# Pooled attention and two MoE layers in one kernel: another distance, order and buffering of a pair's preparation

## The chip, the cores and the metric

The kernel runs on one core of a Trainium2 chip. Its engines are TensorE (PE, with PEld its weight loads), VectorE (DVE), ScalarE (ACT) and GpSimd (POOL); SyncE (SP) issues the transfers (DMAs). Each engine works through its own list of instructions in order and waits at the first whose inputs or buffers aren't ready. The metric is the device time of one execution in microseconds (us), the median of several runs.

## The reference

```python
def _attn_ref(q, k, v):                       # [4, 8, 1152, 64] each
    q_pool = q.reshape(B, H, S // 2, 2, D).mean(axis=3)
    scores = scale * np.matmul(q_pool, k.transpose(0, 1, 3, 2))
    scores = scores - np.max(scores, axis=-1, keepdims=True)
    attn = np.exp(scores)
    attn = attn / (np.sum(attn, axis=-1, keepdims=True) + 1e-09)
    return np.matmul(attn, v)                 # -> x [2304, 512]

def _moe_ref(x, w_in, w_out):                 # 512 -> 2048 -> 512
    h = x @ w_in
    return (h - np.tanh(h)) @ w_out

def _moe2_ref(x, w_in, w_out, s, b):
    r = np.maximum(x @ w_in, 0.0)
    return (s * (r * r) + b) @ w_out
```

All inputs are float32. The output is _moe2_ref of _moe_ref of the attention.

## The kernel before

The 32 heads are worked in 16 pairs, n = 0 to 15, and in a pair the heads j = 0 and 1 follow one another. A head has nine key tiles t of 128 keys, and its 576 pooled queries are two halves g of 288. Keys and queries are kept as a rounded high part and a low remainder, so one tile of scores s is two matmuls: the high parts (L343, operands T1 and U1) and the cross terms together with minus the row's maximum (L344, operands T2 and U2; the last row of U2 is −max, tile c). ACT takes the exponential into pf (L345). After every three tiles a batch of 12 matmuls pv adds pf times values (L412); the sum of pf over keys is made on TensorE in pairs 0 to 3 (su, L378), and afterwards mostly on GpSimd, which adds tiles of pf into acc (L399), with a short su at the end (L425).

Before a pair is scored, the generator prep(n) makes its operands. It adds pairs of queries (L258, on GpSimd after pair 0), transposes queries (ptq, L263) and keys (ptk, L280) on TensorE, copies the results to U1 and T1 on ACT and takes the low parts ql and kl on VectorE. The two heads come out of the transposes one above the other, so halves are moved by DMA: U1 (L275, L276), T1 (L289) and the low parts of the keys into T1 (L290, L291, "T<-kl"). After a pause of GAP ticks come the maxima: 27 tiles of products ptm (L304, L305, L308), each reduced by VectorE (L309), then a reduction over the partial maxima m, a transpose ptc (L313) and a copy with sign changed to c (L314). prep_head(n, j) fills U2, T2 and the values vo by DMA (L324 to L326) and, when c is there, its row of U2 (L332, L334, "U<-c").

The order of the work comes from ticks. The main loop steps through pairs, heads and tiles; every tile has four ticks, a pair 72, and at each tick every prep in the list goes on to its next yield. A scheduler then fixes each engine's list from the order in which instructions were written and from their priorities. Beside the attention stand conversions of the MoE weights on VectorE and GpSimd (L189 to L204), and from pair 5 on matmuls of the first MoE layer (h, L478; y, L491), which fill TensorE. Tiles of scores have three PSUM buffers, and ptq, ptk, ptm and ptc share three others. Behind the attention, from about 700 us, stand the rest of the first MoE layer (L651, L662) and the second (L651, L724).

Of the kernel before, what the change touches and what calls it, by code (L numbers as in the profile page):

```python
# [52 lines left out]
def attention_moe_moe_kernel(  # L53
# [196 lines left out]
    def prep(n):  # L250

        T1, Uz, ql = T1s[n % 2], U1s[n % 2], qls[n % 2]
        U1 = [Uz[j][:, QOFF[j]:QOFF[j] + SQ] for j in range(2)]
        ops[n] = (T1, U1)

        for j in range(2):
            eng = dve if n == 0 else pool
            eng.tensor_add(qr[:, :, 0, j * D:(j + 1) * D], qr[:, :, j, 0:D], qr[:, :, j, D:2 * D])  # L258
        yield 4
        for g in range(2):  # L260
            pt = psP.tile([P, KB], F32, tag="pp", name=f"ptq{n}_{g}")
            for i in range(3):
                nc.tensor.transpose(  # L263
                    pt[:, i * QP:(i + 1) * QP],
                    qr[:, 3 * g + i, 0],
                    ident[:QP, :QP],
                )
            act(U1[1][:, g * HB:(g + 1) * HB], pt[:, :HB], AF.Copy)
            yield 1
            dve.tensor_sub(  # L270
                ql[:, g * HB:(g + 1) * HB], pt[:, :HB], f32(U1[1][:, g * HB:(g + 1) * HB])
            )
            yield 1
        for i in range(2):
            dma(out=f32(U1[0][i * D:(i + 1) * D, :]), in_=f32(U1[1][0:D, :]))  # L275
        dma(out=f32(U1[1][0:D, :]), in_=f32(U1[1][D:P, :]))  # L276
        for g in range(NKB):
            pt = psP.tile([P, KB], F32, tag="pp", name=f"ptk{n}_{g}")
            for i in range(3):
                nc.tensor.transpose(  # L280
                    pt[:, i * P:(i + 1) * P],
                    kr[:, 3 * g + i].rearrange("p h d -> p (h d)"), ident)
            act(T1[1][:, g * KB:(g + 1) * KB], pt, AF.Copy)
            yield 1
            dve.tensor_sub(
                kl[:, g * KB:(g + 1) * KB], pt, f32(T1[1][:, g * KB:(g + 1) * KB])
            )
            yield 1
# [497 lines left out]
```

## Time and profile before

| | |
|---|---|
| median of 3 runs | 1451.95 us (1451.56 to 1452.4) |
| profiled execution | 1451.74 us |
| its span in the trace | 1450.0 us |
| mean granted TensorE clock, whole span | 0.978 |
| busy: PE, DVE, ACT, POOL | 1376.4, 869.2, 553.2, 384.0 us |
| share of the span | 95%, 60%, 38%, 26% |

The span is the time from the first to the last instruction that the profiler recorded; the profiled execution's own time holds 1.74 us around it. Busy shares are means over the whole span, and the attention and the MoE stages have different limits. A granted clock of 1.00 is 2.4 GHz and 0.50 is 1.2 GHz; a value between them over a stretch means that part of it ran at either.

### The profile page before, as it was taken

Reading aid. Unit: us, or ns where it says so; the run is one execution under the profiler, and the core shown is the slowest. Engines: PE = TensorE matmul, PEld = TensorE weight load, DVE = VectorE, ACT = ScalarE, POOL = GpSimd, SP = SyncE. Lnnn points to the kernel's source line nnn. Section 1 sums busy time; section 2 is a strip of 40 time slices with the busy share of each in tenths; the row PEclk is TensorE's granted clock in tenths of the full one; section 3 lists DMA queues with packets and bytes.
Section 4 is the critical chain, followed back from the end, with each engine's and each line's share of the span. In section 5 each row is a group of like instructions: output and inputs, shape, how many; then the busy total and the mean of one; then the engine's idle time right before and its main releaser. Section 6 shows DMA issues by size and latency. Waiting matters only on the chain.

```text
span 1450.0 us, 23111 instructions
## 1 busy us (share of the span) xinstructions
PE 1376.4 (95%) x8670; PEld 1157.0 (80%) x8670; DVE 869.2 (60%) x1638; ACT 553.2 (38%) x1360; POOL 384.0 (26%) x311
## 2 busy tenths in 40 slices
PE   5999989999999999999999998899999999999998
PEld 4656656776777777776898997899889989989987
DVE  7967795756656655668797289934973332323332
ACT  2434435544545444444332233333333222223232
POOL 1211145655655555555221033100220000000000
PEclk9989989999999999999999999999999999999999
DMA  8656654645557535544688044644612020201000
GB/s 200 166 133 152 164 131 116 148 120 116 148 127 168 119 96 127 118 120 114 204 263 263 2 139 149 205 143 149 208 60 66 0 66 0 66 4 62 1 22 22
DMA packets 157647, 169.62 MB, mean 117 GB/s; under 512 B 52064, under 2 KB 130016, under 8 KB 157536
## 3 DMA queue, kind: packets, MB, share of 16 engines
q1 hardware_dynamic: 157536, 168.15, 42.6%
q8 instruction: 68, 1.11, 0.3%
q14 instruction: 43, 0.35, 0.1%
HBM read 101.98 MB, written 30.67 MB: 91 GB/s over the span
## 4 chain that ended last, share of the span: by engine, by line
PE 71%; DVE 16%; DMA 8%; issue 2%; ACT 2%; POOL 1%; SPq 1%; DVEq 0%; ACTq 0%; POOLq 0%
PE h L651 19%; PE o L724 14%; PE pv L412 8%; PE ptm L308 6%; PE y L662 5%; PE s L344 4%; PE s L343 4%; PE y L491 3%; PE h L478 3%; DVE t L193 2%; DMA T<-kl 2%; DVE t L189 2%; DMA raw<-in_moe_w_in_dram 2%; DVE t L191 2%; PE su L425 2%
## 5 line engine op out<-in xcount | busy, mean ns | idle before, releaser
L651 PE MATMUL h<-xx,w 128*128 128x288 f32 (+1 forms) x2328 | 388.4, 316 | 1.8 <-DVE thb L505 1.7
L651 PEld LDWEIGHTS h<-xx,w 128*128 128x128 f32 x2328 | 365.6, 189 | 11.0 <-DVE thb L505 2.7
L309 DVE TENSOR_REDUCE mp<-ptm 128x1 f32<-128x384 f32 x432 | 220.4, 548 | 169.9 <-PE ptm L308 162.3
L345 ACT ACTIVATE pf<-s 128x288 f32<-128x288 f32 x576 | 218.8, 411 | 201.8 <-PE s L344 194.9
L204 POOL TENSOR_TENSOR w<-t,w 128x512 fp32r<-128x512 f32 (+1 forms) x82 | 96.3, 1175 | 371.4 <-ACT w L203 282.9
L662 PE MATMUL y<-ghb,w 128*128 128x288 f32 x784 | 174.9, 297 | 13.6 <-DVE yr L670 9.5
L724 PE MATMUL o<-w,g2h 128*128 128x512 f32 x576 | 180.6, 395 | 0.0
L399 POOL TENSOR_TENSOR acc<-acc,pf 128x576 f32<-128x576 f32 x115 | 165.6, 1440 | 51.5 <-ACT pf L345 46.2
L343 PE MATMUL s<-U,T 128*128 128x288 f32 x576 | 174.4, 312 | 2.9 <-ACT pf L345 1.9
L344 PE MATMUL s<-U,T 65*128 65x288 f32 x576 | 170.2, 306 | 1.5 <-DMA U<-c 1.5
L412 PE MATMUL pv<-pf,vo 128*64 128x288 f32 x1152 | 169.1, 431 | 0.0
L308 PE MATMUL ptm<-T,U 128*128 128x384 f32 x384 | 144.2, 412 | 25.2 <-DMA T<-kl 18.0
L662 PEld LDWEIGHTS y<-ghb,w 128*128 128x128 f32 x784 | 133.0, 190 | 15.4 <-DVE yr L670 10.9
L744 DVE SCALAR_TENSOR_TENSOR r<-r,sb 128x384 f32<-128x384 f32 x96 | 60.1, 626 | 140.1 <-ACT r L743 140.1
L749 DVE SCALAR_TENSOR_TENSOR g2l<-r,sb,g2h 128x384 fp32r<-128x384 f32 x96 | 59.5, 620 | 111.7 <-ACT g2h L748 111.6
L308 PEld LDWEIGHTS ptm<-T,U 128*128 128x128 f32 x384 | 74.1, 201 | 65.1 <-issue 31.2
L343 PEld LDWEIGHTS s<-U,T 128*128 128x128 f32 x576 | 109.3, 190 | 18.6 <-ACT pf L345 10.3
L412 PEld LDWEIGHTS pv<-pf,vo 128*64 128x64 f32 x1152 | 77.0, 141 | 58.6 <-issue 17.0
L662 PE MATMUL y<-glb,w 128*128 128x288 f32 x392 | 117.4, 300 | 4.5 <-DVE glb L509 4.4
L724 PEld LDWEIGHTS o<-w,g2h 128*128 128x128 f32 x576 | 107.3, 188 | 18.0
L344 PEld LDWEIGHTS s<-U,T 65*128 65x128 f32 x576 | 109.9, 192 | 7.4 <-issue 6.1
L724 PE MATMUL o<-w,g2l 128*128 128x512 f32 x288 | 114.1, 396 | 0.0
(78 smaller groups left out, 1722.7 us busy)
## 6 DMA issues: line engine op xcount, KB each, us to landing
xx<-x1d SPq DMA_DIRECT2D x80, 288.0 KB, 3.8
T<-T SPq DMA_DIRECT2D x48, 288.0 KB, 3.4
raw<-in_moe_w_in_dram SPq DMA_DIRECT2D x23, 512.0 KB, 3.7
raw<-in_moe_w_out_dram SPq DMA_DIRECT2D x23, 512.0 KB, 3.5
qr<-in_q_dram SPq DMA_DIRECT2D x32, 288.0 KB, 3.8
kr<-in_k_dram SPq DMA_DIRECT2D x32, 288.0 KB, 4.9
vo<-in_v_dram SPq DMA_DIRECT2D x32, 288.0 KB, 3.8
T<-kl SPq DMA_DIRECT2D x32, 288.0 KB, 3.1
```

Source lines behind the costliest of these rows:

```text
L204: pool.tensor_sub(w[:, 2 * i + 1, cols], x, f32(w[:, 2 * i, cols]))
L308: mm(pt, Uz[j][:, q0:q0 + P], T1[j][:, kk], start=True, stop=True)
L309: dve.reduce_max(mp[:, s, i:i + 1], pt, axis=AX.X)
L343: last[0] = mm(ps, T1[j][:, t * P:(t + 1) * P], U1[j][:, sl], start=True, stop=False)
L344: last[0] = mm(ps, T2[j][:, t * P:(t + 1) * P], U2[j][:, sl], start=False, stop=True)
L345: act(pf[:, sl], ps, AF.Exp, scale=SCALE)
L399: pool.tensor_add(accs[n, j, r], old, pf)
L412: mm(po[g * D:(g + 1) * D], vos[j][:, u], pf[:, g * HB:(g + 1) * HB], start=(t == 0 and i == 0), stop=(u == NKT - BATCH))
L651: mm(ps[:, :n], w[:, a, c * P:(c + 1) * P], xx[:, c, x, 0:n], start=(i == 0 and c == 0), stop=(i == 2 and c == NDC - 1))
L662: mm(ys[i][c], w[:, a, c * P:(c + 1) * P], x, start=(f == fa and r == 0), stop=(f == fb - 1 and r == 2))
L724: mm(ys[i][r], x[:, r * P:(r + 1) * P], w[:, a], start=(f == 0 and n == 0), stop=(f == NFC - 1 and n == 2))
L744: dve.scalar_tensor_tensor(out=r, in0=r, scalar=sb2[:, 0:1], in1=r, op0=ALU.mult, op1=ALU.mult)
```

## The change

The pause before the maxima grows from 12 to 30 ticks (12 stay for pair 1). The prep of pair n+2 starts at tile 4 of head 1 of pair n; before, the prep of pair n+1 started with pair n. The operands T1 and U1 get three sets, used by n modulo 3. The loaded queries lie in one tile for each head. The transposes with their copies and remainders are written with a priority 40 steps earlier. The query additions are tied behind the last traced GpSimd instruction (a subtraction of the weights or an accumulation), and U1's last move, the second move of kl and the transfers of prep_head are tied behind the first move of kl. The exponentials have ten tiles in place of twelve.

```diff
-GAP = 12
+LEAD = 20
+GAP = 30
+GAP1 = 12
+PFB = 10
+SOON = 40
...
+    moved = [None]
+    added = [None]
...
-            pool.tensor_sub(w[:, 2 * i + 1, cols], x, f32(w[:, 2 * i, cols]))
+            added[0] = pool.tensor_sub(w[:, 2 * i + 1, cols], x, f32(w[:, 2 * i, cols]))
...
     T1s = [[pl_.tile([P, S], F32R, name=f"T1_{i}_{j}") for j in range(2)]
-           for i, pl_ in enumerate((pp, ap))]
+           for i, pl_ in enumerate((ap, pp, pp))]
...
-    qr = pp.tile([QP, NQJ, 2, 2 * D], F32, name="qr")
+    qrs = [pp.tile([QP, NQJ, 2 * D], F32, name=f"qr{j}") for j in range(2)]
...
-            dma(out=qr[:, :, j, :], in_=q[b, h0 + j].rearrange("(t p r) d -> p t (r d)", p=QP, r=2))
+            dma(out=qrs[j], in_=q[b, h0 + j].rearrange("(t p r) d -> p t (r d)", p=QP, r=2))
...
-        T1, Uz, ql = T1s[n % 2], U1s[n % 2], qls[n % 2]
+        T1, Uz, ql = T1s[n % 3], U1s[n % 3], qls[n % 2]
...
-            eng.tensor_add(qr[:, :, 0, j * D:(j + 1) * D], qr[:, :, j, 0:D], qr[:, :, j, D:2 * D])
+            with tc.issue_after(added[0].ins) if n > 1 else ExitStack():
+                eng.tensor_add(qrs[0][:, :, j * D:(j + 1) * D], qrs[j][:, :, 0:D], qrs[j][:, :, D:2 * D])
         yield 4
         for g in range(2):
-            pt = psP.tile([P, KB], F32, tag="pp", name=f"ptq{n}_{g}")
...
+            with tc.high_priority(offset=SOON):
+                pt = psP.tile([P, KB], F32, tag="pp", name=f"ptq{n}_{g}")
...
-        dma(out=f32(U1[1][0:D, :]), in_=f32(U1[1][D:P, :]))
         for g in range(NKB):
...
+            with tc.high_priority(offset=SOON):
+                pt = psP.tile([P, KB], F32, tag="pp", name=f"ptk{n}_{g}")
...
         dma(out=f32(T1[0][0:D, :]), in_=f32(T1[1][0:D, :]))
-        dma(out=f32(T1[0][D:P, :]), in_=f32(kl[0:D, :]))
-        dma(out=f32(T1[1][0:D, :]), in_=f32(kl[D:P, :]))
+        moved[0] = dma(out=f32(T1[0][D:P, :]), in_=f32(kl[0:D, :]))
+        with tc.issue_after(moved[0].ins):
+            dma(out=f32(U1[1][0:D, :]), in_=f32(U1[1][D:P, :]))
+            dma(out=f32(T1[1][0:D, :]), in_=f32(kl[D:P, :]))
         if n + 1 < len(pairs):
             later(LOAD, lambda: load_pair(n + 1))
-        yield GAP
+        yield GAP1 if n == 1 else GAP
...
-        dma(out=f32(U2[j][0:D, :]), in_=f32(ql[j * D:(j + 1) * D, :]))
-        dma(out=f32(T2[j][0:D, :]), in_=f32(T1[j][j * D:(j + 1) * D, :]))
-        dma(out=vos[j], in_=v_of(n, j))
+        with tc.issue_after(moved[0].ins) if moved[0] else ExitStack():
+            dma(out=f32(U2[j][0:D, :]), in_=f32(ql[j * D:(j + 1) * D, :]))
+            dma(out=f32(T2[j][0:D, :]), in_=f32(T1[j][j * D:(j + 1) * D, :]))
+            dma(out=vos[j], in_=v_of(n, j))
...
-        pf = ap.tile([P, SQ], F32, tag="pf", name=f"pf{n}_{j}_{t}", bufs=12)
+        pf = ap.tile([P, SQ], F32, tag="pf", name=f"pf{n}_{j}_{t}", bufs=PFB)
...
-        pool.tensor_add(accs[n, j, r], old, pf)
+        added[0] = pool.tensor_add(accs[n, j, r], old, pf)
...
-        if n + 1 < len(pairs):
-            add_prep(n + 1)
+        if n == 0:
+            add_prep(1)
         for j in range(2):
             for t in range(NKT):
+                if j == 1 and t == NKT - LEAD // 4 and n + 2 < len(pairs):
+                    add_prep(n + 2)
```

Three places show what becomes of the engines' lists. In the names, s2_1_0_0 is the tile of scores of pair 2, head 1, key tile 0, query half 0; ptm3_0_1_2 is a tile of products for the maxima of pair 3, head 0; the last number of a name only counts tiles. The line numbers of the changed kernel are 8 or 9 higher (L343, L344, L308, L313 become L352, L353, L316, L321).

TensorE where head 0 of pair 2 ends and head 1 begins, before:

```order
L343 MATMUL s2_1_0_0_1445<-U1_0_1_146,T1_0_1_142 128x288
L343 MATMUL s2_1_0_1_1452<-U1_0_1_146,T1_0_1_142 128x288
L343 MATMUL s2_1_1_0_1482<-U1_0_1_146,T1_0_1_142 128x288
L308 MATMUL ptm3_0_0_0_1378<-T1_1_0_143,U1_1_0_147 128x384
L308 MATMUL ptm3_0_0_1_1413<-T1_1_0_143,U1_1_0_147 128x384
L308 MATMUL ptm3_0_0_2_1426<-T1_1_0_143,U1_1_0_147 128x384
L308 MATMUL ptm3_0_1_0_1434<-T1_1_0_143,U1_1_0_147 128x384
L308 MATMUL ptm3_0_1_1_1441<-T1_1_0_143,U1_1_0_147 128x384
L308 MATMUL ptm3_0_1_2_1449<-T1_1_0_143,U1_1_0_147 128x384
L308 MATMUL ptm3_0_2_0_1456<-T1_1_0_143,U1_1_0_147 128x384
L344 MATMUL s2_1_0_0_1445<-U2_1_159,T2_1_140 128x288
L344 MATMUL s2_1_0_1_1452<-U2_1_159,T2_1_140 128x288
```

The same place in the changed kernel, from the last tile of head 0 on:

```order
L353 MATMUL s2_0_8_0_1440<-U2_0_163,T2_0_139 128x288
L316 MATMUL ptm3_0_1_1_1444<-T1_0_0_141,U1_0_0_147 128x384
L352 MATMUL s2_0_8_1_1447<-U1_2_0_151,T1_2_0_145 128x288
L353 MATMUL s2_0_8_1_1447<-U2_0_163,T2_0_139 128x288
L352 MATMUL s2_1_0_0_1455<-U1_2_1_152,T1_2_1_146 128x288
L316 MATMUL ptm3_0_1_2_1451<-T1_0_0_141,U1_0_0_147 128x384
L352 MATMUL s2_1_0_1_1462<-U1_2_1_152,T1_2_1_146 128x288
L352 MATMUL s2_1_1_0_1492<-U1_2_1_152,T1_2_1_146 128x288
L316 MATMUL ptm3_0_2_0_1459<-T1_0_0_141,U1_0_0_147 128x384
L316 MATMUL ptm3_0_2_1_1466<-T1_0_0_141,U1_0_0_147 128x384
L353 MATMUL s2_1_0_0_1455<-U2_1_164,T2_1_140 128x288
```

The run of seven ptm between the high-part and the low-part scores of head 1 has become two, and the others stand between the scores of head 0, where also ptc2_1, the transpose of head 1's maxima, now stands, twenty places ahead of s2_1_0_0's second matmul.

TensorE at the same border of pair 4 in the changed kernel:

```order
L316 MATMUL ptm5_0_3_2_2407<-T1_2_0_145,U1_2_0_151 128x384
L312 MATMUL ptm5_0_4_0_2420<-T1_2_0_145,U1_2_0_151 128x384
L313 MATMUL ptm5_0_4_0_2420<-T1_2_1_146,U1_2_1_152 128x384
L312 MATMUL ptm5_0_4_1_2428<-T1_2_0_145,U1_2_0_151 128x384
L313 MATMUL ptm5_0_4_1_2428<-T1_2_1_146,U1_2_1_152 128x384
L312 MATMUL ptm5_0_4_2_2445<-T1_2_0_145,U1_2_0_151 128x384
L313 MATMUL ptm5_0_4_2_2445<-T1_2_1_146,U1_2_1_152 128x384
L321 MATMUL ptc5_0_2461<-ident_75,m5_0_2295 5x128
L316 MATMUL ptm5_1_0_0_2469<-T1_2_1_146,U1_2_1_152 128x384
L353 MATMUL s4_1_0_0_2347<-U2_1_164,T2_1_140 128x288
L353 MATMUL s4_1_0_1_2354<-U2_1_164,T2_1_140 128x288
```

Here eleven ptm tiles stay in a run (ptm5_0_1_2 to ptm5_1_0_0), of which the last five are shown.

TensorE around the query transposes of pair 6 (ptq6), before and in the changed kernel, and GpSimd's list in the changed kernel around the additions that feed them (qr0 is the tile of the added queries):

```order
L343 MATMUL s5_0_1_0_2583<-U1_1_0_147,T1_1_0_143 128x288
L344 MATMUL s5_0_1_0_2583<-U2_0_158,T2_0_139 128x288
L263 MATMUL ptq6_0_2587<-ident_75,qr_149 128x96 x3
L478 MATMUL h0_0_0_2542<-xx0_0_2537,w0_121 128x288
L343 MATMUL s5_0_1_1_2593<-U1_1_0_147,T1_1_0_143 128x288
L344 MATMUL s5_0_1_1_2593<-U2_0_158,T2_0_139 128x288
L478 MATMUL h0_0_0_2542<-xx0_0_2537,w0_121 128x288 x3
```

```order
L421 MATMUL pv4_1_2432<-pf4_1_1_2378,vo1_162 64x288 x2
L421 MATMUL pv4_1_2432<-pf4_1_0_2346,vo1_162 64x288 x2
L352 MATMUL s4_1_4_0_2441<-U1_1_1_150,T1_1_1_144 128x288
L353 MATMUL s4_1_4_0_2441<-U2_1_164,T2_1_140 128x288
L352 MATMUL s4_1_4_1_2454<-U1_1_1_150,T1_1_1_144 128x288
L271 MATMUL ptq6_0_2477<-ident_75,qr0_153 128x96 x3
L353 MATMUL s4_1_4_1_2454<-U2_1_164,T2_1_140 128x288
L352 MATMUL s4_1_5_0_2473<-U1_1_1_150,T1_1_1_144 128x288
```

```order
L408 TENSOR_TENSOR acc4_1_0_2393<-acc4_1_0_2393,pf4_1_2_2395 128x576
L408 TENSOR_TENSOR acc4_1_0_2393<-acc4_1_0_2393,pf4_1_3_2415 128x576
L265 TENSOR_TENSOR qr0_153<-qr0_153 96x6x64
L265 TENSOR_TENSOR qr0_153<-qr1_154 96x6x64
L460 TENSOR_TENSOR xo4_0_2410<-xv4_0_2376,xo4_0_2410 128x288
L408 TENSOR_TENSOR acc4_1_0_2393<-acc4_1_0_2393,pf4_1_4_2440 128x576
```

The transposes have moved from pair 5, head 0, tile 1 to pair 4, head 1, tile 4; the additions stand directly behind the accumulation of tile 3 of that head.

The transfer queue around the moves of pair 3 (T1_1, U1_1 before; T1_0, U1_0 after), before and in the changed kernel:

```order
L275 DMA U1_1_0_147<-U1_1_1_148 64x576 x2
L242 DMA qr_149<-in_q_dram 96x6x128
L276 DMA U1_1_1_148<-U1_1_1_148 64x576
L289 DMA T1_1_0_143<-T1_1_1_144 64x1152
L290 DMA T1_1_0_143<-kl_151 64x1152
L291 DMA T1_1_1_144<-kl_151 64x1152
L455 DMA x1d_0_1_90<-xo1_1_1292 128x1x288 x2
L332 DMA U2_1_159<-c1_155 1x4x128
```

```order
L295 DMA T1_0_0_141<-T1_0_1_142 64x1152
L296 DMA T1_0_0_141<-kl_156 64x1152
L298 DMA U1_0_1_148<-U1_0_1_148 64x576
L299 DMA T1_0_1_142<-kl_156 64x1152
L250 DMA kr_155<-in_k_dram 128x9x64 x2
L333 DMA U2_1_164<-ql0_157 64x576
L334 DMA T2_1_140<-T1_2_1_146 64x1152
L335 DMA vo1_162<-in_v_dram 128x576
L464 DMA x1d_0_1_90<-xo1_1_1313 128x1x288 x2
L341 DMA U2_1_164<-c1_160 1x4x128
```

U1's last move has gone behind the first move of kl, and the transfer of c1 stands behind the transfers of the next head and the loads of keys.

## Rows read from the trace of the kernel before

**Rows 1.** Stretch, its length, busy us of PE, PEld, DVE, ACT, POOL, clock, DMA, GB/s.

```profile
60.00:700.00 640.00, 607.86 (x4005) 445.78 (x4004) 429.70 (x806) 301.94 (x828) 303.40 (x246) 0.96 0.54 132
```

**Rows 2.** The same view, first heads of the ten pairs, and their sum.

```profile
69.70:95.40 25.70, 22.62 (x133) 13.73 (x132) 14.97 (x31) 9.19 (x27) 4.43 (x5) 0.80 0.68 170
113.20:136.80 23.60, 21.74 (x135) 13.31 (x134) 14.80 (x31) 9.29 (x28) 4.46 (x5) 0.86 0.74 175
155.00:178.20 23.20, 21.57 (x133) 13.51 (x132) 14.80 (x31) 9.11 (x27) 4.46 (x5) 0.85 0.70 176
197.20:224.30 27.10, 20.97 (x105) 13.53 (x104) 19.98 (x31) 8.87 (x27) 11.00 (x10) 0.75 0.60 147
...
sum 238.90, PE 218.61 PEld 151.12 DVE 145.87 ACT 102.09 POOL 103.44; mean PE 21.86 PEld 15.11 DVE 14.59 ACT 10.21 POOL 10.34
```

**Rows 3.** The same view, second heads of these pairs, and their sum.

```profile
95.40:113.20 17.80, 17.80 (x136) 12.42 (x135) 17.01 (x42) 8.91 (x26) 3.13 (x4) 1.00 0.39 105
136.80:155.00 18.20, 18.07 (x138) 12.42 (x137) 16.75 (x41) 8.97 (x26) 3.13 (x4) 1.00 0.42 115
178.20:197.20 19.00, 17.99 (x136) 12.39 (x135) 17.76 (x42) 9.05 (x26) 5.83 (x6) 1.00 0.43 114
...
sum 185.80, PE 184.07 PEld 139.01 DVE 139.32 ACT 93.51 POOL 85.44; mean PE 18.41 PEld 13.90 DVE 13.93 ACT 9.35 POOL 8.54
```

**Rows 4.** Groups by line, 0 to 700 us: count, busy us, mean ns, idle before.

```profile
L280 PE MATMUL ptk<-ident,kr 128*128 128x128 f32 x144 | 24.4, 287 | 3.6 <-DVE ql L270 3.0 <-DMA kr<-in_k_dram 0.6
...
L263 PE MATMUL ptq<-ident,qr 96*128 96x96 f32 x96 | 14.4, 263 | 7.4 <-DVE qr L258 6.2 <-DVE mp L309 1.0
```

**Rows 5.** TensorE's waits from 60 to 700 us: total us, times, longest.

```profile
PE ptm L308 <- DMA T<-kl: 12.2, 7, 5.9
PE ptm L308 <- DVE mp L309: 4.6, 7, 2.0
```

**Rows 6.** Timeline of TensorE, 160 to 176 us: start, duration, instructions, idle before.

```profile
160.12 1.68 PE L412 MATMUL pv<-pf,vo 128*64 128x288 f32 x12
...
164.78 1.06 PE L343 MATMUL s<-U,T 128*128 128x288 f32 x3
167.20 3.39 PE L308 MATMUL ptm<-T,U 128*128 128x384 f32 x7 [1.36 <-DMA T<-kl]
...
171.15 2.95 PE L412 MATMUL pv<-pf,vo 128*64 128x288 f32 x12
```

**Rows 7.** Timeline of TensorE, 98 to 99 us.

```profile
98.65 0.34 PE L305 MATMUL ptm<-T,U 128*128 128x384 f32 x1
98.83 0.29 PE L343 MATMUL s<-U,T 128*128 128x288 f32 x1
98.96 0.30 PE L344 MATMUL s<-U,T 65*128 65x288 f32 x1
```

**Rows 8.** Groups by line of VectorE, 0 to 700 us.

```profile
L309 DVE TENSOR_REDUCE mp<-ptm 128x1 f32<-128x384 f32 x432 | 220.4, 548 | 169.9 <-PE ptm L308 162.3 <-PE ptm L305 5.1
```

**Rows 9.** Timeline of TensorE, 212 to 220 us.

```profile
212.41 4.79 PE L308 MATMUL ptm<-T,U 128*128 128x384 f32 x10 [5.87 <-DMA T<-kl]
```

**Rows 10.** The tile c (−max): ns min/median/max; its transfers from issue to landing.

```profile
L314 ACT ACTIVATE c<-ptc x32: 249/266/268, 26.5 to 661.5; 5x128 fp32r<-5x128 f32 x16, 4x128 fp32r<-4x128 f32 x16
L332 SPq DMA_DIRECT2D U<-c x32: 655/665/836, 26.7 to 661.8; - x32
...
DMA to landing us min/median/max: 1.6/1.7/3.2
```

**Rows 11.** Timeline of the transfer queue, 160 to 171 us.

```profile
166.62 1.59 SPq L455 DMA_DIRECT2D x1d<-xo  x2
```

**Rows 12.** Groups by line of GpSimd, 0 to 700 us.

```profile
L399 POOL TENSOR_TENSOR acc<-acc,pf 128x576 f32<-128x576 f32 x115 | 165.6, 1440 | 51.5 <-ACT pf L345 46.2
...
L258 POOL TENSOR_TENSOR qr<-qr 96x384 f32<-96x384 f32 x30 | 30.3, 1011 | 69.4 <-DMA qr<-in_q_dram 38.5 <-PE s L344 22.5 <-DMA U<-U 5.7
```

**Rows 13.** Page, part 6: transfer, count, KB, median us from issue to landing.

```profile
T<-kl SPq DMA_DIRECT2D x32, 288.0 KB, 3.1
```

More of the change, by code (lines that the diff above doesn't have):

```diff
@@ L218, in attention_moe_moe_kernel @@
     T1s = [[pl_.tile([P, S], F32R, name=f"T1_{i}_{j}") for j in range(2)]
-           for i, pl_ in enumerate((pp, ap))]
+           for i, pl_ in enumerate((ap, pp, pp))]
     U1s = [[pl_.tile([P, NU], F32R, name=f"U1_{i}_{j}") for j in range(2)]
-           for i, pl_ in enumerate((pp, ap))]
-    qr = pp.tile([QP, NQJ, 2, 2 * D], F32, name="qr")
+           for i, pl_ in enumerate((ap, pp, pp))]
+    qrs = [pp.tile([QP, NQJ, 2 * D], F32, name=f"qr{j}") for j in range(2)]
     kr = pp.tile([P, NKT, 2, D], F32, name="kr")
@@ L230, in attention_moe_moe_kernel @@
         dve.memset(f32(T2[j][D:D + 1, :]), 1.0)
-    for i in range(2):
+    for i in range(3):
         dve.memset(f32(U1s[i][0][:, SQ:]), 0.0)
@@ L257, in prep @@
             eng = dve if n == 0 else pool
-            eng.tensor_add(qr[:, :, 0, j * D:(j + 1) * D], qr[:, :, j, 0:D], qr[:, :, j, D:2 * D])
+            with tc.issue_after(added[0].ins) if n > 1 else ExitStack():
+                eng.tensor_add(qrs[0][:, :, j * D:(j + 1) * D], qrs[j][:, :, 0:D], qrs[j][:, :, D:2 * D])
         yield 4
         for g in range(2):
-            pt = psP.tile([P, KB], F32, tag="pp", name=f"ptq{n}_{g}")
[L262 to L266, printed above, removed]
-                )
@@ L268, in prep @@
[L268 to L273, printed above, removed]
+            with tc.high_priority(offset=SOON):
+                pt = psP.tile([P, KB], F32, tag="pp", name=f"ptq{n}_{g}")
+                for i in range(3):
+                    nc.tensor.transpose(
+                        pt[:, i * QP:(i + 1) * QP],
+                        qrs[0][:, 3 * g + i],
+                        ident[:QP, :QP],
+                    )
+                act(U1[1][:, g * HB:(g + 1) * HB], pt[:, :HB], AF.Copy)
+                dve.tensor_sub(
+                    ql[:, g * HB:(g + 1) * HB], pt[:, :HB], f32(U1[1][:, g * HB:(g + 1) * HB])
+                )
@@ L274, in prep @@
+            yield 2
         for i in range(2):
             dma(out=f32(U1[0][i * D:(i + 1) * D, :]), in_=f32(U1[1][0:D, :]))
-        dma(out=f32(U1[1][0:D, :]), in_=f32(U1[1][D:P, :]))
         for g in range(NKB):
[L278 to L288, printed above, removed]
+            with tc.high_priority(offset=SOON):
+                pt = psP.tile([P, KB], F32, tag="pp", name=f"ptk{n}_{g}")
+                for i in range(3):
+                    nc.tensor.transpose(
+                        pt[:, i * P:(i + 1) * P],
+                        kr[:, 3 * g + i].rearrange("p h d -> p (h d)"), ident)
+                act(T1[1][:, g * KB:(g + 1) * KB], pt, AF.Copy)
+                dve.tensor_sub(
+                    kl[:, g * KB:(g + 1) * KB], pt, f32(T1[1][:, g * KB:(g + 1) * KB])
+                )
@@ L289, in prep @@
+            yield 2
         dma(out=f32(T1[0][0:D, :]), in_=f32(T1[1][0:D, :]))
-        dma(out=f32(T1[0][D:P, :]), in_=f32(kl[0:D, :]))
-        dma(out=f32(T1[1][0:D, :]), in_=f32(kl[D:P, :]))
+        moved[0] = dma(out=f32(T1[0][D:P, :]), in_=f32(kl[0:D, :]))
+        with tc.issue_after(moved[0].ins):
+            dma(out=f32(U1[1][0:D, :]), in_=f32(U1[1][D:P, :]))
+            dma(out=f32(T1[1][0:D, :]), in_=f32(kl[D:P, :]))
         if n + 1 < len(pairs):
             later(LOAD, lambda: load_pair(n + 1))
-        yield GAP
+        yield GAP1 if n == 1 else GAP
```

## The prediction

> **What bounds the kernel now.** I first read the busy times of the stretch that holds the attention from its fourth head on [rows 1]: TensorE is busy 607.86 of 640.00 us and none of the others more than 430, so time can only come from TensorE's own gaps and its own speed. The granted clock there is 0.96: 2 × 0.04 × 640 = 51 us at the lower of its two levels (1.2 instead of 2.4 GHz).
>
> Next I cut the attention at the first value product of every head (pv, L412) and set the two heads of a pair side by side. In ten pairs (1 to 4, 6, 7, 10, 11, 13, 14) the stretch of head 0 is the longer: 238.90 us together [rows 2] against 185.80 us for head 1 [rows 3], whose clock is 1.00 throughout. Both compute the same, except that the next pair's transposes stand in head 0. They cost 14.4 + 24.4 = 38.8 us on TensorE in 16 pairs [rows 4], 2.4 us a pair. So 238.90 − 185.80 − 10 × 2.4 = 29.1 us are lost where head 0 ends. Pairs 5, 8, 9 and 12 show no such loss.
>
> What is lost there, the waits of TensorE tell [rows 5]: the maxima's products (ptm) wait 12.2 us in 7 places for the move of the keys' low parts (T<-kl), and 4.6 us for VectorE's maxima. One place in the timeline, pair 2 to 3, shows the rest [rows 6]: after three scores of head 1 TensorE stands 1.36 us, then issues seven ptm in 3.39 us, 0.48 us each; the next twelve pv take 2.95 us where the same twelve took 1.68 us a few us earlier. Where ptm stand between scores they come every 0.18 us, and scores every 0.13 to 0.14 [rows 7]. So the run of ptm goes at VectorE's pace (a maximum is 548 ns, [rows 8]), and the gap plus this series is followed by the half clock. Worst is pair 4: 5.87 us of standing, then ten ptm in 4.79 us [rows 9].
>
> **The change part by part.** *More distance (GAP, LEAD, SOON, three operand sets).* A pair takes (238.90 + 185.80)/10 = 42.5 us for 72 ticks, 0.59 us a tick. From the moves to the first ptm there were 12 ticks, 7 us; there are now 30, 18 us. The largest lateness seen is 5.87 us, so a further 11 us covers all seven. In the order of the changed kernel, ptm of pair n+1 begin at tile 6 of head 0 of pair n, one after each two scores, where TensorE before had a run of seven at the head's border. That removes the waits, the runs and, where nothing else stops TensorE, the half clock: 29.1 us. What stays of it:
> - Pair 4 keeps a run: eleven tiles of ptm ahead of the first low-part score of head 1. At 0.48 instead of 0.18 us that is 11 × 0.30 = 3.3 us; some half clock behind it, as in [rows 6] (2.95 − 1.68 = 1.3 us a batch of pv), about 1.7: 5 us.
> - Pairs 8 and 12 keep runs of three: 2 × 3 × 0.30 = 1.8 us if VectorE had nothing in hand; three result tiles are buffered, so I take 1.
>
> *A new wait for the second head's maxima.* The row −max of head 1 used to be copied long before its use; now ptc of head 1 stands between tiles 6 and 7 of head 0, and the path from it is: transpose 0.27 [rows 4], ACT's copy 0.27, the transfer's issue 0.67 and its landing 1.7 [rows 10], 2.9 us; with two x1d issues ahead of it in the queue, 1.59 us [rows 11], 4.5 us. TensorE has in that time, in the order, eight ptm and twelve scores: 8 × 0.18 + 12 × 0.13 = 3.0 us at its own pace, 8 × 0.48 = 3.8 at VectorE's. The wait is then 0 (no x1d ahead) to 1.5 us a pair, in 14 pairs 0 to 21 us. I take 2 us in all, near the lower end, since the x1d pair is sent once a head and must fall just there to count. Behind that wait stand the twelve pv of the last batch, which would otherwise run.
>
> *Query additions behind an accumulation.* Before, the two additions stood late enough that the transposes (ptq) had their inputs. Now they are tied behind the last accumulation or subtraction on GpSimd, and ptq stands in TensorE's order at tile 4 of head 1; TensorE issues in order, so every score behind ptq waits too. In pair 4, GpSimd does the accumulation of tile 3 (1.44 us) and both additions (2 × 1.01) [rows 12] after tile 3's exponential, with half of an accumulation in hand (0.7, my estimate): 0.7 + 1.44 + 2.02 = 4.2 us. TensorE has a batch of pv and three scores for it: 1.68 + 3 × 0.14 = 2.1 us. The wait is 2.1 us. Pairs 8 and 12 have about 1 us more work between (1.1 us of wait each). In the others 5 us and more of TensorE's work stand between: nothing. Sum 4.3 us. Its bounds are 0 (GpSimd is ahead) and 2.1 in each of 13 pairs, 27.3.
>
> *Two tiles for the queries.* The same two additions of the same size; the load of head 1's queries no longer waits for the other's. Loads land well ahead: nothing; if that cover went, an addition's 1.0 us once a pair would show in the wait above.
>
> *Order of the transfers.* The move of U1's lower half (0.46 us of issue) goes behind T<-kl, so T<-kl leaves that much earlier; it lands in 3.1 us [rows 13], now hidden by the 18 us. U2, T2 and vo of the next head are held behind that move as well; they are issued some 20 ticks, 12 us, ahead of their use. Nothing; without the cover 1 us of issue a pair.
>
> *Ten instead of twelve exponential tiles.* ACT is busy 102.09 of 238.90 us in [rows 2], so it has time to catch up; nothing. If the cover went, ACT would wait for one accumulation, 1.44 us, where GpSimd is behind.
>
> *Start.* Pair 1 keeps the distance 12; one more memset of zeros, one addition less on the path: between −0.5 and +0.5 us, I take 0. Behind the attention the order of the MoE stages is the same: 0.
>
> **Sum.** 29.1 − 5 − 1 − 2 − 4.3 = 16.8 us, against the profiled execution's 1451.74 (span 1450.0 and 1.74 around it): 1434.9, so 1435. The median of the runs is 1451.95, 0.2 above that execution, which changes nothing.
>
> **Rivals.**
> - *A: much of the half clock returns.* Of 29.1 us, 12.2 are the waits for T<-kl; the other 16.9 are ptm at VectorE's pace and the half clock. A gap of 1.36 us and a run of 3.4 us sufficed for it in [rows 6], and the new waits (ptq, −max) are of that size. If half of 16.9 stays: 16.8 − 8.4 = 8.4, 1443. Against it: the heads in [rows 3] hold 1.00 with gaps of some 1 us (178.20: 17.99 busy of 19.00).
> - *B: VectorE becomes the bound in pairs 1 to 4.* In their second heads it is busy 17.01 of 17.80 us [rows 3], and the maxima now begin earlier but are no fewer. If the whole gain of pairs 1, 2 and 3 (25.7 − 17.8 − 2.4 = 5.5; 23.6 − 18.2 − 2.4 = 3.0; 23.2 − 19.0 − 2.4 = 1.8) goes: 16.8 − 10.3 = 6.5, 1445. Against it: their first heads have VectorE at 14.97 of 25.70, so there is room to spread into.
> - *C, slower: TensorE's first query transpose waits for GpSimd in every pair.* Place: ptq at tile 4 of head 1, at the 2.1 us of pair 4, in 13 pairs 27.3 instead of 4.3: 1434.9 + 23 = 1458. It decides from (16.8 + 4.3)/13 = 1.6 us a pair. For it: the tie is the same in all pairs, and TensorE is the engine that stands. Against: only from pair 4 on is GpSimd filled with accumulations (11.00 us in 197.20 to 224.30, 4.43 in 69.70 to 95.40, [rows 2]), and in most pairs other TensorE work lies between in the order.
> - *D: the change doesn't do what it says.* The runs go, but −max of head 1 takes their place in all pairs at its upper 1.5 us (21 instead of 2): 16.8 − 19 = −2, 1454, no change that a measurement shows. For it: head 1's scores stand in order behind it. Against: the start of that path is on ACT and SP, neither of which is full.
> - *E: the half clock costs half of its time.* 51 us [rows 1] at half speed would be 25.5 us; with 12.2 + 4.6 of waits 42.3, less 12.3 (5 + 1 + 2 + 4.3): 30.0, 1422. Against: that is more than the 29.1 us by which the stretches are longer, since in part of that time TensorE stands, or goes at VectorE's pace and would not be faster. "TensorE: Matmul & The Clock Gate" of the Trainium skill, section "HAM oscillation — how this bites in real kernels", prices throttled time so, the whole of it times one minus the clock's ratio. The rows disagree in size: the comparison of heads, waits included, leaves no room for the full price.
>
> **How the numbers follow.** My forecast has 0.58 with a range of its own from 1425 (both new waits nothing, pair 4's run half as dear: 29.1 − 2.5 = 26.6) to 1441 (new waits 10 more between them). A 0.14 (1443), B 0.08 (1445), C 0.08 (1458), D 0.08 (1454), E 0.04 (1422). The range of 8 in 10 leaves out C, D and at most half of E and ends at 1422 and 1449. Less than 0.2%, 2.9 us, is about what a measurement of this kernel can't tell from no change. Faster: 0.58 + 0.14 + 0.08 + 0.04 = 0.84; the same: D, 0.07 of it; slower: C and the rest of D, 0.09.
>
> **What the profile after would show.** Right: in the waits of TensorE T<-kl is gone from ptm; the first heads of the ten pairs are at about 20 to 22 us with clock 1.00, the clock of the whole stretch at 0.99; only pair 4 has a run of ptm at 0.48 us. The second term: s (now L353) waits for U<-c about 2 us. The third: ptq waits for the added queries 2.1 us in pair 4, 1 us in 8 and 12, nothing elsewhere. Wrong: clock below 1.00 at each head's border (A); VectorE without a gap in pairs 1 to 4 while ptm wait for mp (B); ptq's wait in all pairs (C); U<-c over 10 us (D).

## The result, and the profile after

The changed kernel took 1429.35 us (median of 4 runs, 1426.25 to 1431.43) against 1451.76 for the kernel before in the same comparison: a ratio of 0.9848 with a 95% interval of 0.9825 to 0.987, 22.4 us less. The forecast was 1435, its range 1422 to 1449. The profiled execution took 1429.16 us, its span is 1427.4. One execution of a later run, e8, took 4523 us and is left out of that run's ratio.

The attention now ends near 669 us, where it ended near 691, so nearly all of the difference lies there. The first two lines are the stretch from 60 us to that end, before and after (columns as in [rows 1]); the second fence is to [rows 5], TensorE's waits in it after the change:

```profile
60.00:691.00 631.00, 598.86 (x3943) 438.18 (x3943) 422.04 (x788) 298.36 (x819) 301.35 (x243) 0.96 0.54 131
60.00:669.00 609.00, 581.66 (x3938) 438.12 (x3936) 415.83 (x788) 303.94 (x817) 302.34 (x243) 0.97 0.55 136
```

```profile
PE ptm L316 <- DVE mp L317: 10.8, 8, 2.9
PE ptq L271 <- POOL qr L265: 9.0, 3, 3.5
PE su L434 <- POOL acc L408: 2.9, 1, 2.9
PE ptc L321 <- DVE m L319: 2.7, 4, 1.0
PE s L353 <- DMA U<-c: 1.1, 1, 1.1
```

The wait for T<-kl, 12.2 us before, is gone. In its place stand two others: ptq for the query additions, 9.0 us in exactly three places, and more waiting for VectorE's maxima, 10.8 instead of 4.6 us. So the waits hardly shrink in sum: TensorE stands 27.3 us of the stretch instead of 32.1. The greater part of the gain is in its busy time, 17.2 us less. One share of that is the clock: added up over the trace, 31 us of the stretch are at half clock, where it was 51. Another share shows in pair 10, which has the same matmuls of the first MoE layer in both kernels and no half clock. Its two heads before (first fence) and after (second), by the view of [rows 2]:

```profile
447.60:488.80 41.20, 40.40 (x269) 30.83 (x268) 24.11 (x44) 19.86 (x55) 24.00 (x19) 1.00 0.60 147
```

```profile
437.80:476.70 38.90, 38.90 (x270) 30.62 (x269) 25.50 (x45) 20.45 (x55) 23.57 (x19) 1.00 0.67 166
```

TensorE was busy nearly throughout and the clock 1.00 in both, yet the pair became 2.3 us shorter. The run of seven ptm at its border in the kernel before, on the timeline of TensorE, shows most of it:

```profile
461.18 0.88 PE L308 MATMUL ptm<-T,U 128*128 128x384 f32 x3
462.24 1.84 PE L308 MATMUL ptm<-T,U 128*128 128x384 f32 x4 [0.18 <-DVE mp L309]
463.92 0.43 PE L344 MATMUL s<-U,T 65*128 65x288 f32 x2
```

From the first start to that of the next score the seven take 2.74 us, where seven at 0.18 [rows 7] would take 1.26: 1.5 of the 2.3 us. The last four take 1.84 us, 0.46 each, at VectorE's pace: its maxima start 0.46 to 0.47 us apart there, though each lasts 0.55. My comparison of heads gave this pair a loss of only 22.3 − 18.9 − 2.4 = 1.0 us. The record of one ptm lasts longer than the time to the next start (0.34 us against 0.18 in [rows 7]; 0.44 to 0.45 against 0.46 in this run), so products that are held to 0.46 us still show as busy, and neither the busy share nor the table of waits shows this loss.

The new wait of ptq in pair 4, on TensorE's and then GpSimd's timeline of the changed kernel:

```profile
217.68 0.30 PE L352 MATMUL s<-U,T 128*128 128x288 f32 x1
221.51 0.74 PE L271 MATMUL ptq<-ident,qr 96*128 96x96 f32 x3 [3.53 <-POOL qr L265]
```

```profile
214.96 1.42 POOL L408 TENSOR_TENSOR acc<-pf,pf 128x576 f32<-128x576 f32 x1 [8.19 <-ACT pf L354]
216.45 2.99 POOL L408 TENSOR_TENSOR acc<-acc,pf 128x576 f32<-128x576 f32 x2
219.40 2.05 POOL L265 TENSOR_TENSOR qr<-qr 96x384 f32<-96x384 f32 x2
```

GpSimd stood 8.19 us and then got the exponentials of a batch almost at once; three accumulations, 4.4 us, stood ahead of the additions, not the one and a half that I had reckoned with.

The wait for maxima begins in the transfer queue. In pair 1, the queue, then VectorE, then TensorE:

```profile
74.32 0.61 SPq L335 DMA_DIRECT2D vo<-in_v_dram  x1
79.31 1.22 SPq L464 DMA_DIRECT2D x1d<-xo  x2
80.91 0.68 SPq L341 DMA_DIRECT2D U<-c  x1
82.61 0.53 SPq L333 DMA_DIRECT2D U<-ql  x1
83.19 0.59 SPq L334 DMA_DIRECT2D T<-T  x1
83.83 0.58 SPq L181 DMA_DIRECT2D raw<-in_moe_w_out_dram  x1
```

```profile
87.99 0.29 DVE L195 TENSOR_SCALAR t<-raw 128x256 int32<-128x256 int32 x1 [3.27 <-DMA raw<-in_moe_w_out_dram]
```

```profile
92.13 0.44 PE L316 MATMUL ptm<-T,U 128*128 128x384 f32 x1 [2.91 <-DVE mp L317]
```

The load of raw weights stands behind transfers that wait for their inputs; VectorE, which issues in order, stands 3.27 us at the conversion; the maxima behind that conversion, itself 3.5 us of work, come late, and TensorE stands 2.91 us. VectorE's waits from 60 to 250 us hold 13.4 us of this kind, where the same stretch before had 0.7:

```profile
DVE t L195 <- DMA raw<-in_moe_w_out_dram: 8.3, 4, 4.1
...
DVE t L195 <- DMA raw<-in_moe_w_in_dram: 5.1, 1, 5.1
```

### The profile page after: what moved, and what is told of

Read it like the earlier page. It is cut to its first block, busy times and chain, and to the rows that moved or that the text cites. A ratio compares the mean times of both kernels' runs of the same rounds, so it can differ in the third digit from the quotient of the medians.

```text
span 1427.4 us, 23107 instructions
## 1 busy us (share of the span) xinstructions
PE 1359.7 (95%) x8670; PEld 1157.2 (81%) x8670; DVE 865.0 (61%) x1640; ACT 559.6 (39%) x1360; POOL 385.5 (27%) x311
## 4 chain that ended last, share of the span: by engine, by line
PE 72%; DVE 16%; DMA 5%; POOL 3%; issue 3%; ACT 1%; SPq 1%; DVEq 0%; POOLq 0%; ACTq 0%
PE h L662 19%; PE o L735 14%; PE pv L421 9%; PE ptm L316 5%; PE y L673 5%; PE s L352 4%; PE s L353 4%; PE y L500 3%; PE h L487 2%; DVE t L199 2%; DMA raw<-in_moe_w_out_dram 2%; DVE t L197 2%; DVE mp L317 2%; DVE t L195 2%; POOL acc L408 2%
## 5 line engine op out<-in xcount | busy, mean ns | idle before, releaser
L317 DVE TENSOR_REDUCE mp<-ptm 128x1 f32<-128x384 f32 x432 | 225.2, 549 | 128.7 <-PE ptm L316 118.9
L352 PE MATMUL s<-U,T 128*128 128x288 f32 x576 | 177.2, 314 | 0.6
L353 PE MATMUL s<-U,T 65*128 65x288 f32 x576 | 173.4, 309 | 1.1 <-DMA U<-c 1.1
L421 PE MATMUL pv<-pf,vo 128*64 128x288 f32 x1152 | 165.0, 423 | 0.0
L316 PE MATMUL ptm<-T,U 128*128 128x384 f32 x384 | 141.6, 387 | 16.6 <-DVE mp L317 10.8
L421 PEld LDWEIGHTS pv<-pf,vo 128*64 128x64 f32 x1152 | 75.6, 139 | 59.6 <-ACT pf L354 10.6
L352 PEld LDWEIGHTS s<-U,T 128*128 128x128 f32 x576 | 111.6, 194 | 14.4 <-ACT pf L354 6.8
L353 PEld LDWEIGHTS s<-U,T 65*128 65x128 f32 x576 | 111.6, 194 | 5.9 <-issue 4.5
L759 ACT ACTIVATE g2h<-r,sb 128x384 fp32r<-128x384 f32 x96 | 59.5, 620 | 125.4 <-PE o L735 110.1
```

What stands on the lines that cost most here:

```text
L316: mm(pt, Uz[j][:, q0:q0 + P], T1[j][:, kk], start=True, stop=True)
L317: dve.reduce_max(mp[:, s, i:i + 1], pt, axis=AX.X)
L352: last[0] = mm(ps, T1[j][:, t * P:(t + 1) * P], U1[j][:, sl], start=True, stop=False)
L353: last[0] = mm(ps, T2[j][:, t * P:(t + 1) * P], U2[j][:, sl], start=False, stop=True)
L421: mm(po[g * D:(g + 1) * D], vos[j][:, u], pf[:, g * HB:(g + 1) * HB], start=(t == 0 and i == 0), stop=(u == NKT - BATCH))
```

## The experiments

Ratios are to the kernel before in the same comparison, with 95% intervals; the changed kernel's is 0.9848.

**e1: query additions of three pairs on VectorE.**

```diff
-            eng = dve if n == 0 else pool
+            eng = dve if n == 0 or n in (6, 10, 14) else pool
```

(Their tie to GpSimd's last instruction goes with them.)

> The changed kernel with the query additions of pairs 6, 10 and 14 on VectorE instead of GpSimd. Theory (the additions queued behind GpSimd's accumulations hold TensorE): the three waits of ptq for POOL qr, 9.0 us together in the changed kernel, go, and with them the three half-clock stretches that follow them (6.8, 3.4 and 6.8 us, worth up to 8.5 us): 1429 - 9 - (3 to 8) = 1412 to 1417. Rival 1 (another wait steps in at the same place, since the loads or VectorE are as late): 1426 to 1430. Rival 2 (the clock costs nothing by itself): 1420.

1411.6 us, 0.9736 (0.9711 to 0.976): 17.8 less than the changed kernel. The theory holds. The three pairs, 4, 8 and 12, in the changed kernel and in e1, by the view of [rows 2]:

```profile
195.10:238.50 43.40, 38.37 (x226) 27.03 (x225) 27.51 (x52) 18.87 (x52) 23.97 (x20) 0.92 0.63 148
352.30:400.80 48.50, 44.97 (x297) 36.12 (x296) 27.85 (x50) 20.90 (x58) 25.17 (x20) 0.96 0.64 161
514.00:563.60 49.60, 46.04 (x297) 36.78 (x296) 27.83 (x50) 20.87 (x57) 25.14 (x20) 0.93 0.63 157
sum 141.50, PE 129.38 PEld 99.93 DVE 83.20 ACT 60.64 POOL 74.28; mean PE 43.13 PEld 33.31 DVE 27.73 ACT 20.21 POOL 24.76
```

```profile
193.70:230.90 37.20, 35.72 (x225) 24.92 (x225) 27.49 (x53) 18.07 (x51) 22.57 (x18) 1.00 0.68 166
344.10:387.80 43.70, 43.13 (x298) 34.68 (x297) 27.46 (x49) 19.93 (x57) 22.21 (x18) 1.00 0.73 173
501.00:544.60 43.60, 43.02 (x296) 34.61 (x295) 27.41 (x49) 19.88 (x55) 22.14 (x18) 1.00 0.71 174
sum 124.50, PE 121.88 PEld 94.20 DVE 82.36 ACT 57.88 POOL 66.92; mean PE 40.63 PEld 31.40 DVE 27.45 ACT 19.29 POOL 22.31
```

They become 17.0 us shorter, 9.0 of waits and 8.0 more. The clock goes from 0.92, 0.96 and 0.93 to 1.00: 2 × (0.08 × 43.4 + 0.04 × 48.5 + 0.07 × 49.6) = 18 us at half clock by these rounded clocks (17.1 by the trace's own stretches of 6.8, 3.4 and 6.8 us) cost about 8.

**e2: without the tie of the additions.**

```diff
-            with tc.issue_after(added[0].ins) if n > 1 else ExitStack():
+            with ExitStack():
```

> The changed kernel without the tie of the query additions to GpSimd's last instruction; on GpSimd's list they then stand behind the accumulation of tile 7 or 8 in most pairs from 5 on, while ptq stands at tile 5 or 6 in TensorE's. Theory (place on GpSimd's list decides whether ptq waits): ptq waits one to two tiles (2.1 us each) plus two additions in about ten pairs, 3 to 5 us each, less the 3.5 us of pair 4: 1429 + 27 to 45 = 1456 to 1474. Rival (GpSimd runs ahead of its list's place, the tie does nothing): 1427 to 1431.

1420.91 us, 0.9792 (0.9768 to 0.9816). My expectation was wrong in its reading of the list: the additions behind tile 7 of a pair are those of a pair later, so without the tie they come a head earlier, not later. The waits of ptq for GpSimd are gone from the view, as in e1, so the tie made them; the theory that the place on the list decides is kept, the number was the wrong way round. e2 stays 9.3 us behind e1: accumulations now come late, and su waits 6.8 us for them instead of 2.9. That is 3.9 us; the rest is not explained.

**e3: the pause at 12 again.**

```diff
-GAP = 30
+GAP = 12
```

> The changed kernel with the pause before the maxima at 12 ticks again; start of the preparation, three operand sets and the order of the moves stay. Theory A (the distance from the moves to the maxima gives the gain): waits of ptm for T<-kl come back, 1 to 2 us in 7 to 15 pairs with some half clock behind: 1440 to 1452. Theory B (that the maxima stand before the heads' border, which the early start gives, is what counts): T<-kl waits fall between scores and are short, 1426 to 1433.

1428.14 us, 0.9839 (0.9814 to 0.9864), the same as the changed kernel. Theory B: the larger distance is not what gives the gain. No wait for T<-kl stands in this stretch, though the maxima of pairs from 6 on begin three tiles earlier than in the changed kernel. The equal time is a sum of unequal parts: ptq waits 3.5 instead of 9.0 us for the additions, and VectorE's waits for raw weights from 60 to 250 us are gone, but the scores now wait 6.3 us for exponentials, and pair 4 is 5.9 us longer.

**e4: fewer conversions in pairs 0 to 3.**

```diff
-CONVERT = (4, 4, 4, 4, 2, 2, 0, 0, 0, 1, 1, 1, 1)
+CONVERT = (3, 3, 3, 3, 4, 4, 0, 0, 0, 1, 1, 1, 1)
```

> The changed kernel with 3 instead of 4 steps of weight conversion in each of pairs 0 to 3 and 4 instead of 2 in pairs 4 and 5. Theory (VectorE is the bound in pairs 0 to 3, where ptm waits for its maxima, 10.8 us in 8 places): a step is some 2.7 us of VectorE, so up to 10.8 us less there, and 0 to 4 us more in pairs 4 and 5: 1418 to 1424. Rival (VectorE has slack over the pair, the waits are those of three result buffers): 1428 to 1431; if the first MoE products wait for later weights, over 1433.

1426.82 us (1420.91 to 1429.23), 0.9824 (0.9799 to 0.9849): not told apart from the changed kernel, and between the two expectations. ptm's wait for the maxima falls from 10.8 to 6.6 us, but ptc then waits 6.1 instead of 2.7: most of what pairs 1 to 3 win, pairs 5 and 6 lose.

**e5: the preparation starts as late as before, pause 12.**

```diff
-        if n == 0:
-            add_prep(1)
+        if n + 1 < len(pairs):
+            add_prep(n + 1)
...
-                if j == 1 and t == NKT - LEAD // 4 and n + 2 < len(pairs):
-                    add_prep(n + 2)
```

> The changed kernel with the start of the preparation as before (prep of pair n+1 at the start of pair n) and the pause at 12 ticks; the third operand set, the order of the moves, the ties and the priority of the transposes stay. On TensorE's list the maxima then begin at tile 1 of head 1 again, in a run, and ptq is far behind its additions. Theory (the early start counts, because it brings the maxima out of the run at the head's border and between scores): most of the gain goes, 1440 to 1452. Rival (the order of the moves, the ties and the priority bring the keys' low parts in time and give the gain): 1415 to 1430.

1465.4 us, 1.0099 (1.0075 to 1.0123): slower than the kernel before, by more than the theory said. With the late start TensorE waits for the moved keys again, although the moves' order, the ties, the priority and the third set are all there:

```profile
PE ptm L316 <- DMA T<-kl: 14.4, 4, 5.0
PE s L353 <- DMA T<-T: 3.3, 3, 1.7
```

e3 differs from this run in the start alone and is 37 us faster. The early start is what carries the change; with the late start the other parts cost 14.6 us.

**e6: the kernel before, its maxima over half of the keys.**

```diff
-                    dve.reduce_max(mp[:, s, i:i + 1], pt, axis=AX.X)
+                    dve.reduce_max(mp[:, s, i:i + 1], pt[:, :KB // 2], axis=AX.X)
```

> The kernel before with each maximum taken over 192 of its 384 keys (the other half of the keys is left out of the maxima); everything else stays. A maximum on VectorE then takes some 0.3 instead of 0.55 us. Theory (a large part of what the change won is ptm at VectorE's pace, 2.2 us in every pair, the pairs without a visible loss too): 15 x 2.2 = 33 us less, plus some half clock, less what the transfers' 12.2 us still hold: 1412 to 1428. Rival (what the change won is the waits for the moved keys and the half clock behind them, VectorE's pace is small): 1442 to 1450.

1425.37 us, 0.9824 (0.98 to 0.9848): 25.4 less, with a maximum at 350 instead of 548 ns. So the length of a maximum decides over about as much time as the whole change won, and the rival's time is missed by far. But this is not VectorE's pace alone: the wait for T<-kl fell as well, from 12.2 to 5.1 us, and the half-clock time of the attention from 51 to 14 us. In the seven pairs without half clock in either run (5, 6, 8, 9, 10, 12 and 14) the pairs became 0.3 to 1.7 us shorter, 8.9 us together. That much is the pace by itself, in pairs without a large wait too; how the rest divides between the pace, the waits and the clock behind them is not shown.

**e7: U1's move in its old place, and no ties of transfers.**

```diff
+        dma(out=f32(U1[1][0:D, :]), in_=f32(U1[1][D:P, :]))
         for g in range(NKB):
...
-        with tc.issue_after(moved[0].ins):
-            dma(out=f32(U1[1][0:D, :]), in_=f32(U1[1][D:P, :]))
-            dma(out=f32(T1[1][0:D, :]), in_=f32(kl[D:P, :]))
+        dma(out=f32(T1[1][0:D, :]), in_=f32(kl[D:P, :]))
...
-        with tc.issue_after(moved[0].ins) if moved[0] else ExitStack():
+        with ExitStack():
```

> The changed kernel with U1's last move in its old place ahead of the keys' moves, and without the ties of that move, of the second move of kl and of the next head's transfers. Theory (the distance covers the transfers, their order is worth nothing): 1427 to 1432. Rival (the order keeps the moves of kl out of the queue behind others; without it ptm wait for T<-kl again): 1435 to 1445.

1411.82 us, 0.973 (0.9706 to 0.9754). Neither theory: the order of the transfers isn't worth nothing, it costs 17.5 us. This part of the change works against the rest (e9 shows where).

**e8: e1 with conversions moved to pair 4.**

```diff
-CONVERT = (4, 4, 4, 4, 2, 2, 0, 0, 0, 1, 1, 1, 1)
+CONVERT = (4, 4, 3, 3, 4, 2, 0, 0, 0, 1, 1, 1, 1)
```

> Run e1 (query additions of pairs 6, 10 and 14 on VectorE, 1411.6) with one step of weight conversion less in each of pairs 2 and 3 and two more in pair 4. Theory (VectorE is the bound in pairs 1 to 3, has room in pair 4; with the steps moved in e4, pairs 2 and 3 became 3.3 and 4.5 us shorter): 1404 to 1408. Rival (what pairs 2 and 3 gain comes back in pairs 4 and 5): 1410 to 1413.

1416.12 us, 0.9756 (0.9732 to 0.9781), no better than e1. With fewer conversions in pairs 2 and 3, VectorE's waits for raw weights (13.2 us) and ptm's for VectorE (11.2) stay as they were. In e4, where the waits for weights fell to 2.6 us, pairs 1 to 3 became 10.0 us shorter. So in these pairs late weights count for more than the number of conversions. They are not all: in e3 VectorE had no such wait, and ptm still waited 7.9 us for the maxima.

**e9: only the tie of the next head's transfers taken away.**

```diff
-        with tc.issue_after(moved[0].ins) if moved[0] else ExitStack():
+        with ExitStack():
             dma(out=f32(U2[j][0:D, :]), in_=f32(ql[j * D:(j + 1) * D, :]))
```

> The changed kernel without the tie of the next head's transfers (U2, T2, vo) behind the first move of kl; U1's last move stays behind it. Theory (that tie puts transfers which wait long ahead of the loads of weights in the queue, VectorE stands for the weights, TensorE for VectorE's maxima; and ptq of pairs 10 and 14 moves half a tile later without it): all of what e7 won, 1409 to 1415. Rival (the place of U1's move is what e7 won): 1426 to 1431.

1415.33 us, 0.9758 (0.9735 to 0.9782), 14.0 less: most of e7, and its interval overlaps that of e7. VectorE's waits for raw weights from 60 to 250 us are halved (6.7 instead of 13.4), ptm's for the maxima go from 10.8 to 7.0 and ptq's from 9.0 to 4.3, since the ptq of pairs 10 and 14 now stand half a tile later. Both ways were expected, and the stretches of the pairs separate them. Pairs 1 to 3, then pairs 8 and 12, each first in the changed kernel and then in e9:

```profile
sum 125.10, PE 115.92 PEld 77.19 DVE 95.37 ACT 57.14 POOL 22.50; mean PE 38.64 PEld 25.73 DVE 31.79 ACT 19.05 POOL 7.50
sum 114.50, PE 111.61 PEld 75.30 DVE 90.32 ACT 56.69 POOL 19.59; mean PE 37.20 PEld 25.10 DVE 30.11 ACT 18.90 POOL 6.53
```

```profile
sum 98.10, PE 91.01 PEld 72.90 DVE 55.69 ACT 41.77 POOL 50.31; mean PE 45.50 PEld 36.45 DVE 27.84 ACT 20.89 POOL 25.15
sum 87.80, PE 85.81 PEld 69.04 DVE 56.25 ACT 42.51 POOL 50.41; mean PE 42.91 PEld 34.52 DVE 28.12 ACT 21.25 POOL 25.21
```

Pairs 1 to 3, where the waits for weights and maxima shrink, become 10.6 us shorter. Pairs 8 and 12, where ptq's waits go, become 10.3 us shorter. Pairs 5 and 6 become 5.0 us longer (81.5 instead of 76.5). So a large part of what this tie costs is the same waits for additions that e1 takes away, by another way, and the gains of e1, e7 and e9 can't be added.

**e10: e7 with the additions of pair 6 on VectorE.** (The edit of e1 for n = 6 alone.)

> Run e7 (moves and ties of transfers as before, 1411.8) with the query additions of pair 6 on VectorE, since e7 kept one wait of ptq for them, 3.9 us with 6.8 us of half clock behind. Theory (the two costs are separate and add): 3.9 + 3 = 7 us less, 1403 to 1407. Rival (another wait takes its place): 1410 to 1413.

1408.7 us, 0.9707 (0.9684 to 0.9729). The last wait of ptq is gone from the view, but 3 of the expected 7 us came, and the intervals of e7 and e10 overlap. That the two costs add is not borne out: ptc waits 4.8 us for VectorE instead of 3.1.

**e11: the changed kernel, its maxima over half of the keys.** (The edit of e6.)

> The changed kernel with each maximum over 192 of its 384 keys (half of the keys is left out of the maxima), as e6 for the kernel before, where it gave 25.4 us. Theory (the change has taken most of VectorE's pace out of TensorE's list; what is left is the stalls for weights, for GpSimd's additions, and one run of ptm in pair 4): 5 to 10 us, 1419 to 1424. Rival (VectorE's pace still holds TensorE in every pair): 15 to 25 us, 1404 to 1414.

1409.67 us, 0.972 (0.9698 to 0.9743), 19.7 less: the size of the rival, not its place. By the stretches of the pairs, pairs 6, 10 and 14 keep their length within 0.6 us; the gain lies in pairs 1 to 4 and in 8 and 12, where ptq's waits also moved. How much VectorE's pace alone still costs stays open.

**e12: e10 with three buffers for raw weights.**

```diff
-                    2, 2, 2, LAST_STEPS)
+                    2, 3, 2, LAST_STEPS)
```

> Run e10 with three instead of two buffers for the raw weights of the first conversions, so that each load is issued one conversion step (some 4 us) earlier. Theory (VectorE still stands for late weights, 7.3 us in pairs 1 to 5 in e10, and TensorE for its maxima, 5.9 and 4.8 us): VectorE's waits for raw nearly go, TensorE's halve: 3 to 7 us less than e10, 1401 to 1406. Rival (VectorE makes up for it elsewhere; pairs 1 to 3 are bound by its work): 1407 to 1410.

1406.01 us (1400.29 to 1406.76), 0.9673 (0.9645 to 0.9701), the fastest version: 23 us below the changed kernel. VectorE's wait for raw weights falls to 2.6 us and ptm's for it from 5.9 to 4.1. The step from e10 is 2.7 us where 3 to 7 were expected, and its interval overlaps that of e10.

## Why the prediction was right, and where not

The time and the direction came out (22.4 us for 16.8), by two errors that partly cancel.

- *The gain, 29.1 us, was too small.* The step that failed is "both compute the same, except that the next pair's transposes stand in head 0". The products ptm in the ten first heads and in the ten second heads of the kernel before, with the columns of [rows 2] for this tile alone:

```profile
sum 238.90, PE 47.67; mean PE 4.77
```

```profile
sum 185.80, PE 61.76; mean PE 6.18
```

  By count these are 117 and 186 products. The second heads, my measure of a head without loss, held 69 more (12.4 us at 0.18), and 36 matmuls of the MoE layer less (about 4.7 us at 0.13). That hid some 8 us of the first heads' loss. The transposes hid more. ptk stood in the first heads alone (first line), but ptq mostly in the second ones (second line the first heads, third line the second heads):

```profile
sum 238.90, PE 14.48; mean PE 1.45
sum 238.90, PE 2.64; mean PE 0.26
sum 185.80, PE 5.22; mean PE 0.52
```

  The first heads thus had 14.5 + 2.6 − 5.2 = 11.9 us more of transposes and not the 24 that I subtracted. Set right, the comparison gives a loss of about 29.1 + 7.7 + 12.1 = 49 us in place of 29.1. With e10 as the change without most of its own new costs, the gain is 1451.1 − 1408.7 = 42 us. The kind of loss was right: read from start to start, the eleven runs of four or more ptm from 60 us on (74 products) took some 22 us more than at 0.18 us each before the change, waits and clock inside them included, and the three that are left (25 products) some 3.5. Of the pairs that "show no such loss", 8 and 12 had such a run, of four at 0.38 us; 5 and 9 had none.
- *The places.* The total hides that the gain fell elsewhere. Pairs 1 to 4 together, before and after:

```profile
sum 171.10, PE 157.26 PEld 104.06 DVE 127.72 ACT 72.12 POOL 47.81; mean PE 39.31 PEld 26.02 DVE 31.93 ACT 18.03 POOL 11.95
sum 168.50, PE 154.30 PEld 104.22 DVE 122.89 ACT 76.01 POOL 46.48; mean PE 38.57 PEld 26.06 DVE 30.72 ACT 19.00 POOL 11.62
```

  They became 2.6 us shorter. By the prediction's own terms they had 18.5 of the 29.1 us to gain, 11.4 after pair 4's run and its wait for the additions. Pairs 5 to 15 became 19.5 us shorter, where the sum had some 7. That the total came out to 6 us is in this respect luck.
- *The distance.* That T<-kl waits go was right; that 12 against 30 ticks do it was not (e3). The early start does (e5).
- *−max of head 1:* forecast 2 us in all, measured 1.1 in one place. Right.
- *The additions behind an accumulation:* right in mechanism and in each of the three places (pairs 4, 8, 12), mis-sized: 9.0 us of waits for 4.3, and 8 us of half clock behind them, which the sum left out (e1).
- *Order of the transfers:* costed at nothing with the 18 us as cover. That covers the moves themselves, but not what is queued behind them. The ties cost 14 us or more (e7, e9), in pairs 1 to 3, where VectorE waits for weights, and in pairs 8 and 12, where ptq comes earlier against its additions. I had not followed the queue to VectorE's conversions.
- *Pair 4's run:* forecast 5 us. It is there at full clock; on the timeline its first seven ptm take 2.82 us, and ptc waits 0.98 behind them. Smaller than forecast, some 3 us: 11 × (0.40 − 0.18) + 1.
- *Rivals.* B came in its place, pairs 1 to 4, though not in the total: ptm waits 10.8 us for the maxima, in part because weights come late (e9) and not by the number of conversions (e8). C's wait came in three pairs, not thirteen. D fell. Of A, the half clock did return behind the new waits: the stretch has 0.97, where 0.99 was the sign of being right. My premise there, that "the gap plus this series" is followed by the half clock, was misread in [rows 6], the border of pair 3, where the run of seven begins at 167.20 us and the clock has fallen before it, in the gap (the clock is the third figure from the end, 1.00 and then 0.50):

```profile
163.50:166.95 3.45, 2.29 (x11) 1.50 (x10) 1.83 (x5) 1.43 (x4) 1.59 (x2) 1.00 0.68 153
166.95:170.40 3.45, 3.19 (x8) 2.00 (x8) 2.50 (x6) 0.00 (x0) 0.00 (x0) 0.50 0.71 174
```

  On E: the 17.1 us at half clock in e1's three pairs cost 8.0, 0.47 us each. "TensorE: Matmul & The Clock Gate" of the Trainium skill, section "HAM oscillation — how this bites in real kernels", gives half. There the trace nearly agrees, and my rejection of that price rested on the faulty comparison; the sum of E was still further from 1429.35 than my own.
- *Ten exponential tiles, two query tiles:* costed at nothing and not tried alone.
